# Memory attention and long convolution in one kernel: two stages in series against one program ordered by a build-time list scheduler

## The chip, the cores and the metric

One core of a Trainium2 chip runs the whole kernel. The metric is device time in microseconds (us) for one execution, smaller being better. TensorE is the matmul engine; VectorE and ScalarE do elementwise work; GpSimd does a few fills; SyncE (SP) issues every DMA transfer. In the profile these are PE (PEld for weight loads), DVE, ACT, POOL and SP.

## The reference, cut to what matters

`x` has 2048 tokens of 512 features. One branch is attention with 32 heads of 16 features in 4 segments of 512 tokens: causal softmax inside a segment, plus a linear-attention memory of the earlier segments. The other is a convolution of every feature with its own 2048-tap kernel, the sum of 128 complex exponentials. A sigmoid gate per token mixes the two.

```python
for s in range(4):
    logits = einsum('bhqd,bhkd->bhqk', qs, ks) * scale + mask      # causal
    a_dot = einsum('bhqk,bhkd->bhqd', softmax(logits), vs)
    a_mem = einsum('bhld,bhde->bhle', phi(qs), M) / (einsum('bhld,bhd->bhl', phi(qs), z)[..., None] + 1e-06)
    outs.append(g * a_mem + (1.0 - g) * a_dot)
    M, z = M + einsum('bhld,bhle->bhde', phi(ks), vs), z + phi(ks).sum(l)
a = concat(outs) @ wo
l = arange(2048).astype(bfloat16)          # lags above 256 are rounded
K = einsum('dn,dnl,dn->dl', C, exp(dt * A * l), dt * B).real
b = irfft(rfft(pad(u, 4096)) * rfft(pad(K, 4096)))[:2048] + u * Dskip
return gate * a + (1 - gate) * b           # u = x; gate = sigmoid(x . gate_w)
```

The lags `l` are rounded to bfloat16, so many of the 2048 taps of a feature's kernel are equal.

## The kernel before, in words

Each engine has a list of instructions, filled by Python code in the order in which they are to run. `EngQ.add` appends an instruction with the semaphore counts that it waits for, and `KB.dma` (L107) appends a transfer to SP's list. An engine runs its list in order. The attention is written out first, wholly, then `ssm_pipeline`.

**Loads and projections.** The constants come first in SP's list, with 32 small transfers of the output weights, and then the four transfers of `x`. L295 transposes `x`, 64 blocks of 128x128. `proj_qk` (L332, L348) and `proj_v` (L363, L374) make q, k, v and the feature-mapped k, 240 matmuls of 512 columns. L434 sums the memory of the segments.

**Attention.** 64 pairs of heads (4 segments, 4 head groups, 4 pairs) run one after the other. For a pair, `emit_qk` makes the lower triangle of the scores by 128-row blocks, 8 matmuls (L544, L559) that use 32 rows of the array each, the two heads in different row strips. `emit_exp` takes the exponential with three ACT instructions (L572 and L574 of 1024 columns, L576 of 512) and multiplies the four diagonal blocks of each head by a 0/1 mask on DVE (L582, L585). `emit_pv` makes the weighted sums, 8 matmuls with 17 columns of weights (L608), two heads in different column strips. L618 takes the result of four heads out of PSUM. The normalisation (L632 to L663) and the output projection (L674, 128 matmuls of 512 columns over a zero-padded weight) are held in a list of steps, `deferred`, and one or two of them follow each pair.

**Convolution.** `ssm_pipeline` starts its loads when the attention is done (`attn_done`). It makes the per-step factors from the parameters (L843 to L868) and the powers that squaring gives (`powers`, L908 to L922, DVE). Then it runs over 4 chunks of 128 features:

- `tables_gen`: in 4 quarters of 32 features, a table F of 65 powers and a table G of 32 powers, doubled level by level with 6 DVE instructions (L880 to L885), and a pair of matmuls per feature (L992, L996) that contracts the 128 states and gives the kernel at 65 x 32 lags. L1252 takes it out of PSUM, and L1006 and L1027 copy it to rounded lags on DVE.
- `fft_front`: 128 matmuls of 64 columns (L1068) for kernel and for `x`, the second transform level (L1099, 64 columns a matmul), the product of the two spectra (L1120 to L1124 on DVE), the first inverse level (L1137).
- `bounce_read`: the result goes to DRAM and back with another layout, six transfers a chunk. Two have 32 rows outermost, two have 31, two fill one partition each.
- `fft_back`: the last inverse level (L1190), then on DVE the skip term (L1206, L1207) and the gate (L1210, L1212, 128 columns an instruction).

```python
a1 = DV.add(lambda e: e.tensor_tensor(dst_r, src_r, mrb, ALU.mult), deps=deps)                     # L880, one of six
for c in range(4):
    ...
    gen = tables_gen(c + 1) if c + 1 < 4 else None
    ...
    fft_front(c, gen, ...)
    ...
    bounce_read(c)
fft_back(3)
```

So the tables of the next chunk run beside the transform of this one, and nothing of the convolution runs beside the attention.

Of the kernel before, what the change touches and what calls it, by code (L numbers as in the profile page):

```python
# [8 lines left out]
BF16 = mybir.dt.bfloat16  # L9
F32 = mybir.dt.float32  # L10
U16 = mybir.dt.uint16

DEBUG = {}

S = 2048; D = 512; H = 32; DH = 16; NSEG = 4; LSEG = 512; NST = 128
NEG = -30000.0
NDMA_SEMS = 48
NDUMMY = 0
HOOK = False
# [9 lines left out]
class Tok:  # L29
    __slots__ = ("sem", "val")  # L30

    def __init__(self, sem, val):
        self.sem = sem
        self.val = val


class EngQ:
    def __init__(self, name, sem):
        self.name = name
        self.sem = sem  # L40
        self.count = 0
        self.items = []

    def add(self, fn, deps=(), inc=True):
        deps = [d for d in deps if d is not None]
        tok = None
        if inc:
            self.count += 1
            tok = Tok(self.sem, self.count)
        self.items.append((deps, fn, inc))  # L50
        return tok

    def emit(self, eng):
        waited = {}
        for deps, fn, inc in self.items:
            need = {}
            for d in deps:
                if waited.get(id(d.sem), -1) >= d.val:
                    continue
                if id(d.sem) not in need or need[id(d.sem)].val < d.val:  # L60
                    need[id(d.sem)] = d
            for d in need.values():
                eng.wait_ge(d.sem, d.val)
                waited[id(d.sem)] = d.val
            if fn is None:
                continue
            ins = fn(eng)
            if inc:
                ins.then_inc(self.sem, 1)


class KB:
    def __init__(self, nc, es):
        self.nc = nc
        self.es = es
        self.block = es.enter_context(nc.Block())
        self.nsem = 0
        self.PE = EngQ("pe", self.sem("q_pe"))
        self.AC = EngQ("act", self.sem("q_act"))
        self.DV = EngQ("dve", self.sem("q_dve"))  # L80
        self.PO = EngQ("pool", self.sem("q_pool"))
        self.SP = EngQ("sp", self.sem("q_sp"))
        self.dma_toks = []
        self.dma_rr = 0

    def sem(self, name):
        self.nsem += 1
        return self.es.enter_context(self.nc.semaphore(name))

    def sb(self, name, shape, dt):  # L90
        return self.es.enter_context(self.nc.sbuf_tensor(name, shape, dt))

    def dma(self, out, in_, deps=(), q=None, slow=False):
        q = q or self.SP
        if not hasattr(self, "dpool"):
            self.dpool = [[self.sem("dp%d" % i), 0] for i in range(NDMA_SEMS)]
            self.dnext = 0
        ent = self.dpool[self.dnext % NDMA_SEMS]
        self.dnext += 1
        sem, prev_total = ent  # L100
        deps = [d for d in deps if d is not None]
        if prev_total > 0:
            deps.append(Tok(sem, prev_total))
        ent[1] = prev_total + 16
        t = Tok(sem, ent[1])
        kw = {"allow_slow_non_contiguous": True} if slow else {}
        q.items.append((deps, lambda e, o=out, i=in_, s=sem, kw=kw: e.dma_start(o, i, **kw).then_inc(s, 16), False))  # L107
        self.dma_toks.append(t)
        return t
# [7 lines left out]
    def finish(self):  # L117
        self.SP.items.append(([Tok(sm, tot) for sm, tot in self.dpool if tot > 0], None, False))
        b = self.block
        with self.nc.allow_low_precision("bf16 kernel by design"):  # L120
            self._emit_all(b)
# [1219 lines left out]
```

## Time and profile before

| | us |
|---|---|
| median of 3 runs | 1047.57 (1046.41 to 1048.4) |
| the profiled execution, first to last instruction | 1045.3 |
| PE busy | 550.2 |
| DVE busy | 683.1 |
| ACT busy | 346.7 |

The profiled span is the time from the first to the last instruction of one execution. The device time of a run holds a little more, what lies around that span; the median is 2.3 us above it. Busy is the time in which an engine has at least one instruction under way, so three engines can each be busy at the same time. [...] A row of "x512" stands for 512 instructions.

### The profile page before, as it was taken

The numbers are of one execution on the slowest core, as the hardware profiler recorded it, in microseconds if no ns is written. First come the engines' busy times: TensorE is split into PE (matmuls) and PEld (weight loads), VectorE is DVE, ScalarE is ACT, GpSimd is POOL, SyncE is SP. The second block draws the span as 40 slices with busy tenths as digits, with TensorE's granted clock in tenths as the row PEclk, the third lists the DMA queues.
The fourth block names the chain that finished last, engine by engine and source line by source line (L and its number), as shares of the span: only waits on it lengthen the run. The fifth ranks groups of instructions, "written<-read, shape, count | busy, mean of one in ns | idle before, by whom it ended". The sixth has DMA issues, their size and how long they took to land.

```text
span 1045.3 us, 14554 instructions
## 1 busy us (share of the span) xinstructions
PE 550.2 (53%) x5560; PEld 348.1 (33%) x5560; DVE 683.1 (65%) x2362; ACT 346.7 (33%) x523; POOL 7.2 (1%) x7
## 2 busy tenths in 40 slices
PE   0995687977868845000118562745546651866000
PEld 0543122322222201000107562745436551865000
DVE  0896645555555451799979997999749996422404
ACT  0761377756746301100114232322323322423000
POOL 2000000000000000000000000000000000000000
PEclk9996556585585656555655555555655655555555
DMA  3300000000000003810000000130041300512413
GB/s 99 95 1 1 1 1 1 6 16 1 6 16 1 16 6 74 263 11 1 1 0 3 1 2 1 62 43 1 1 84 38 45 1 6 92 44 58 63 28 62
DMA packets 93486, 32.63 MB, mean 31 GB/s; under 512 B 85704, under 2 KB 92488, under 8 KB 92648
## 3 DMA queue, kind: packets, MB, share of 16 engines
q1 hardware_dynamic: 93416, 31.69, 13.4%
q8 instruction: 44, 0.72, 0.3%
q14 instruction: 26, 0.21, 0.1%
HBM read 23.16 MB, written 8.53 MB: 30 GB/s over the span
## 4 chain that ended last, share of the span: by engine, by line
DVE 52%; PE 24%; ACT 10%; SPq 7%; issue 3%; DMA 3%; POOL 0%; POOLq 0%; DVEq 0%
SPq L107 7%; DVE arenaB L1027 5%; DVE arenaA L885 4%; DVE arenaA L882 4%; DVE arenaA L880 4%; ACT arenaA L572 3%; DVE arenaA L884 3%; PE psum L608 3%; ACT arenaA L574 3%; PE psum L674 3%; PE psum L544 3%; PE psum L1099 3%; DVE scr L883 2%; DVE arenaA L881 2%; DVE arenaA L1120 2%
## 5 line engine op out<-in xcount | busy, mean ns | idle before, releaser
L1137 PE MATMUL psum<-arenaC,arenaB 64*128 64x64 bf16 x528 | 20.7, 237 | 164.2 <-DVE arenaC L1124 164.2
L572 ACT ACTIVATE arenaA<-psum 128x1024 bf16<-128x1024 f32 x64 | 65.5, 1024 | 110.1 <-PE psum L544 110.1
L992 PE MATMUL psum<-arenaA 128*32 128x65 bf16 x512 | 36.3, 325 | 104.5 <-DVE arenaA L943 92.1
L608 PE MATMUL psum<-arenaA,arenaB 128*17 128x512 bf16 (+3 forms) x512 | 74.4, 435 | 16.5 <-DVE arenaA L618 16.5
L896 ACT ACTIVATE arenaC<-psum 128x512 bf16<-128x512 f32 (+1 forms) x72 | 37.9, 555 | 134.8 <-PE psum L1137 117.5
L585 DVE TENSOR_TENSOR arenaA<-arenaA,mask 128x256 bf16<-128x256 bf16 x128 | 36.9, 288 | 66.8 <-ACT arenaA L576 66.8
L1252 ACT ACTIVATE arenaA<-psum 128x455 bf16<-128x455 f32 (+1 forms) x20 | 39.3, 2062 | 106.0 <-PE psum L996 106.0
L1137 PEld LDWEIGHTS psum<-arenaC,arenaB 64*128 64x128 bf16 x528 | 15.0, 122 | 173.9 <-DVE arenaC L1124 173.9
L544 PE MATMUL psum<-arenaB 32*128 32x512 bf16 (+2 forms) x384 | 62.0, 443 | 13.4 <-ACT arenaA L574 10.2
L574 ACT ACTIVATE arenaA<-psum 128x1024 bf16<-128x1024 f32 x64 | 65.1, 1017 | 0.0
L1099 PE MATMUL psum<-arenaC,arenaB 128*128 128x64 bf16 x512 | 63.0, 288 | 0.0
L1099 PE MATMUL psum<-arenaA,arenaB 128*128 128x64 bf16 x512 | 62.5, 287 | 0.0
L1109 ACT ACTIVATE arenaC<-psum 128x512 bf16<-128x512 f32 (+1 forms) x36 | 21.4, 594 | 116.7 <-PE psum L1099 115.4
L1206 DVE TENSOR_TENSOR x4c<-x4c,dskb 128x2048 bf16<-128x2048 bf16 x4 | 4.9, 1225 | 81.7 <-DMA dskb<-in_B_Dskip_dram 81.7
L992 PEld LDWEIGHTS psum<-arenaA 128*32 128x32 bf16 x512 | 22.7, 150 | 106.7 <-DVE arenaA L943 93.0
L1099 PEld LDWEIGHTS psum<-arenaC,arenaB 128*128 128x128 bf16 x512 | 57.1, 122 | 0.0
L582 DVE TENSOR_TENSOR arenaA<-arenaA,mask 128x256 bf16<-128x256 bf16 x128 | 36.6, 286 | 30.9 <-ACT arenaA L572 30.9
L1099 PEld LDWEIGHTS psum<-arenaA,arenaB 128*128 128x128 bf16 x512 | 52.8, 121 | 4.6 <-issue 2.5
L1027 DVE SCALAR_TENSOR_TENSOR arenaB<-arenaA,qmask,arenaB 128x128 bf16<-128x128 bf16 (+2 forms) x112 | 50.1, 447 | 4.0
L880 DVE TENSOR_TENSOR arenaA<-arenaA,arenaB 128x64 bf16<-128x64 bf16 (+5 forms) x176 | 52.1, 296 | 0.0
L882 DVE TENSOR_TENSOR arenaA<-arenaA,arenaB 128x64 bf16<-128x64 bf16 (+5 forms) x176 | 52.1, 296 | 0.0
L1120 DVE TENSOR_TENSOR arenaA<-psum,arenaC 128x512 bf16<-128x512 f32 (+1 forms) x36 | 23.1, 643 | 35.0 <-PE psum L1099 32.8
(145 smaller groups left out, 1248.6 us busy)
## 6 DMA issues: line engine op xcount, KB each, us to landing
arenaB<-c_M2bd SPq DMA_DIRECT2D x1, 4224.0 KB, 16.1
scr_Vd<-arenaC SPq DMA_DIRECT2D x4, 1056.0 KB, 5.0
arenaB<-c_N SPq DMA_DIRECT2D x1, 2112.0 KB, 21.2
arenaA<-in_A_x_dram SPq DMA_DIRECT2D x4, 512.0 KB, 5.1
scr_abuf<-a_sb SPq DMA_DIRECT2D x16, 128.0 KB, 1.7
arenaA<-in_A_x_dram SPq DMA_DIRECT2D x16, 128.0 KB, 4.4
arenaB<-scr_Vd SPq DMA_DIRECT2D x8, 256.0 KB, 3.6
a4c<-scr_abuf SPq DMA_DIRECT2D x16, 128.0 KB, 4.9
```

Source lines behind the costliest of these rows:

```text
L107: q.items.append((deps, lambda e, o=out, i=in_, s=sem, kw=kw: e.dma_start(o, i, **kw).then_inc(s, 16), False))
L544: toks[which] = PE.add(lambda e, r=r, J=J, n=n, off=off, kT_src=kT_src: e.matmul(psum[:, off:off + n], lhsT=kT_src[32 * r:32 * r + 32, hg, ...
L572: tA = AC.add(lambda e, sl=sl: e.activation(pT[:, sl, 0:1024], psum[:, 0:1024], ACT.Exp, scale=0.25), deps=[qt[0]] + pt_readers[sl] + extra)
L574: tB = AC.add(lambda e, sl=sl: e.activation(pT[:, sl + 1, 0:1024], psum[:, 1024:2048], ACT.Exp, scale=0.25), deps=[qt[1]] + pt_readers[sl ...
L608: ms[which].append(PE.add(lambda e, c=c, J=J, n=n, off=off, slot=slot, h=h: e.matmul(bankf(B_ND)[32 * c:32 * c + 17, 128 * J:512], lhsT=vp ...
L880: a1 = DV.add(lambda e: e.tensor_tensor(dst_r, src_r, mrb, ALU.mult), deps=deps)
L882: a4 = DV.add(lambda e: e.tensor_tensor(dst_i, src_r, mib, ALU.mult), deps=deps)
L885: a6 = DV.add(lambda e: e.tensor_tensor(dst_i, dst_i, s2, ALU.add), deps=[a4, a5])
L992: m1 = PE.add(lambda e, o=o, dq=dq, dloc=dloc, Gr=Gr, Fr=Fr, bkm=bkm: e.matmul(bankf(bkm)[32 * dq:32 * dq + 32, o:o + 65], lhsT=Gr[:, :, d ...
L1027: tq_dv.append(DV.add(lambda e, dst=dst, src=src, gi=gi: e.scalar_tensor_tensor(dst, src, qm[:, gi:gi + 1], dst, ALU.mult, ALU.add), deps= ...
L1099: mm = PE.add(lambda e, b=b, p=p, p4=p4, c_in=c_in, c_out=c_out, rho=rho, ci=ci, ncin=len(cins): e.matmul(bankf(b)[:, 256 * c_out + 64 * p ...
L1120: d1 = DV.add(lambda e, KA=KA, n_=n_, xv=xv: e.tensor_tensor(sub_ap(T1, 0, [[256, 2], [1, n_]]), xv, sub_ap(KA, 0, [[256, 2], [1, n_]]), A ...
```

## The change

The whole kernel is written anew. Every instruction, or a closure of several matmuls, is an `Op` with an engine, a modelled cost, the tiles that it reads and writes, and a key. `Sched.schedule` runs over all of them when the kernel is built. On each engine it takes, of the ops whose inputs are there within 0.12 us, the one with the lowest key, and it so fixes one order per engine for attention and convolution together. SBUF tiles come from pools with a fixed number of buffers; a pool that lies over another's memory opens when that one has been given back. In the model a transfer costs SP 0.06 us. Keys: attention group i (of 32) has 6 + 12 i, the tables of chunk c have 50 + 70 c, the last stage starts at 335.

- **Loads**: one small constant, parameters and the first part of `x` stand first in SP's order.
- **Attention**: 32 groups of four heads. A group has five PSUM tiles of 1024 columns, each with one exponential. The diagonal is masked by a further matmul that adds -30000 to the scores; the DVE masks are gone. The memory state uses k's two feature parts as separate matmuls; normalisation works with tokens on partitions, with transposes on PE; the output projection has no padding (64 matmuls instead of 128).
- **Tables**: whole chunks of 128 features, 32 x 49 products that hold each rounded lag once, three DVE instructions a level on real and imaginary part together (15 levels, 78 steps of 256 elements a chunk), powers mostly on ACT. The kernel stays at its distinct lags: it is transposed to 5 x 128 rows, and no copy to 2048 lags is made.
- **Transform**: at odd frequencies. `x`'s first level is made early, with 32 matmuls of 512 columns, and kept in DRAM. In the last stage, 16 steps of 128 frequencies: the kernel's spectrum is a product of a constant matrix (transferred per step) with the distinct lags, 10 matmuls of 512 columns; 16 small matmuls (64x64, 256 columns, four at a time) for `x`; three products on DVE; 4 matmuls of 512 columns back; result to DRAM, and read back 4 steps at a time with 8 partitions a transfer.
- **End**: per block of 128 tokens one matmul for the skip term, two half-height ones for the last level, and one DVE instruction for the gate, 16 times.

```diff
-class EngQ:
-    def add(self, fn, deps=(), inc=True):
...
+    def schedule(self):
...
+                for key, seq, o in lst:
+                    est = te
+                    for d in o.deps:
+                        a = arrive(d, e)
+                        if a > est:
+                            est = a
...
+                    if best is None or est < best[0] - 1e-9:
+                        best = (est, key, seq, o)
+                    if est <= te + SL:
+                        best = (est, key, seq, o)
+                        break
...
+            slots = [[(Ah, 0, 0, 0), (Bh, 0, 1, 0)],
+                     [(Ah, 1, 0, 0), (Bh, 1, 1, 0), (Ah, 3, 0, 384), (Bh, 3, 1, 384)],
+                     [(Ch, 0, 0, 0), (Dh, 0, 1, 0)],
+                     [(Ch, 1, 0, 0), (Dh, 1, 1, 0), (Ch, 3, 0, 384), (Dh, 3, 1, 384)],
+                     [(Ah, 2, 0, 0), (Bh, 2, 1, 0), (Ch, 2, 0, 256), (Dh, 2, 1, 256)]]
...
+                        mm(e, ap(P, bk * 512 + off, n=n), ap(kT, 128 * J, n=128, p0=32 * r, np_=32),
+                           ap(qT, 128 * J, n=n, p0=32 * r, np_=32), len(dg[bk]) == 0, False, tile_position=(32 * r, 0))
...
+                        i = mm(e, ap(P, bk * 512 + d[0], [[st, len(d)], [1, 128]]), ap(ident, n=128),
+                               ap(negm, dims=[[0, len(d)], [1, 128]]), False, True)
...
+                op("ACT", c_act(1024), lambda e, P=P, pT=pT: e.activation(ap(pT, n=1024), ap(P, n=1024), ACT.Exp, scale=0.25), r=[P], w=[pT])
...
+                op("DVE", c_tt(256 * n), lambda e: e.tensor_tensor(
+                    D_(), ap(tile, src * 128, [[pl, 2], [128 * sstep, n], [1, 128]]),
+                    ap(pw, d0, [[0, 2], [0, n], [1, 128]]), ALU.mult), r=rd + [pw], w=wr + [tile])
...
+            for t in range(16):
+                S.key = k0 + 4 + 3.8 * t
...
+                S.dma(lambda Dt=Dt: ap(Dt, n=1280), lambda t=t: hD[t], 327680, w=[Dt], key=S.key - 8)
...
+                        for kt in range(5):
+                            i = mm(e, ap(PK, c * 512, n=512), ap(Dt, kt * 256 + c * 128, n=128), ap(KTT, kt * 512, n=512), kt == 0, kt == 4)
...
+                S.dma(lambda t=t: bass.AP(Vd, t * 131072, [[1024, 128], [1, 1024]]), lambda V=V: ap(V, n=1024), 262144, r=[V], pw=[dV[t // 4]])
+                if t % 4 == 3:
...
+                            S.dma(lambda bl=bl, c=c, k=k: sbp(V2, 64 * bl + 32 * c + k, 4, 8, [[512, 32], [1, 512]]),
...
+                op("DVE", c_dps(512), lambda e, P=P, ou=ou, aj=aj, bl=bl, b4=b4: e.scalar_tensor_tensor(
+                        ap(ou, bl * 512, n=512), ap(P, n=512), ap(omg4T, b4, n=1), ap(aj, bl * 512, n=512), ALU.mult, ALU.add),
...
+        for s in range(4):
+            for hg in range(4):
+                i0 = 8 * s + 2 * hg
...
+                for gi in range(2):
+                    S.key = TA0 + GA * (i0 + gi)
+                    group(s, hg, gi)
...
+        for c in range(4):
+            S.key = TT0 + TT * c
+            tables(c)
...
+        tail(TT0 + 4 * TT + 5)
+        S.schedule()
...
```

## Rows read from the trace of the kernel before

**Rows 1.** The page: busy time of the three engines, share of the span, instructions.

```profile
PE 550.2 (53%) x5560; PEld 348.1 (33%) x5560; DVE 683.1 (65%) x2362; ACT 346.7 (33%) x523; POOL 7.2 (1%) x7
```

**Rows 2.** The page: the chain that ended last, share of the span by engine.

```profile
DVE 52%; PE 24%; ACT 10%; SPq 7%; issue 3%; DMA 3%; POOL 0%; POOLq 0%; DVEq 0%
```

**Rows 3.** Busy time by stage: start:end, length, engines (instructions), PEclk, DMA share, GB/s.

```profile
25.50:84.00 58.50, 57.68 (x324) 28.79 (x323) 52.21 (x96) 38.45 (x68) 0.00 (x0) 1.00 0.15 47
...
112.00:405.50 293.50, 220.57 (x1252) 73.73 (x1250) 147.87 (x377) 155.39 (x192) 0.00 (x0) 0.62 0.02 7
405.50:470.00 64.50, 3.54 (x24) 2.06 (x24) 43.83 (x166) 7.84 (x12) 0.00 (x0) 0.52 0.51 135
470.00:961.70 491.70, 253.25 (x3744) 234.31 (x3744) 400.43 (x1610) 138.62 (x240) 0.00 (x0) 0.54 0.12 23
961.70:1045.30 83.60, 4.61 (x124) 2.50 (x114) 21.62 (x68) 4.78 (x8) 0.00 (x0) 0.50 0.34 64
```

**Rows 4.** Timeline of PE and SP at the start: start, length, what, idle before.

```profile
20.83 2.07 SPq L107 DMA_DIRECT2D arenaA<-in_A_x_dram  x4
...
24.95 5.79 PE L295 MATMUL psum<-ident,arenaA 128*128 128x128 bf16 x64 [24.95 <-DMA arenaA<-in_A_x_dram]
```

**Rows 5.** Groups by line and shape: exponentials and DVE instructions; busy, mean ns.

```profile
L574 ACT ACTIVATE arenaA<-psum 128x1024 bf16<-128x1024 f32 x64 | 65.1, 1017 | 0.0
L576 ACT ACTIVATE arenaA<-psum 128x512 bf16<-128x512 f32 x64 | 38.6, 603 | 0.0
L618 DVE CAST arenaA<-psum 128x512 bf16<-128x512 f32 x32 | 21.9, 684 | 0.5 <-PE psum L608 0.5
L880 DVE TENSOR_TENSOR arenaA<-arenaA,arenaB 128x1024 bf16<-128x1024 bf16 x16 | 11.0, 686 | 0.0
L1206 DVE TENSOR_TENSOR x4c<-x4c,dskb 128x2048 bf16<-128x2048 bf16 x4 | 4.9, 1225 | 81.7 <-DMA dskb<-in_B_Dskip_dram 81.7
L880 DVE TENSOR_TENSOR arenaA<-arenaA,arenaB 128x256 bf16<-128x256 bf16 x32 | 9.2, 287 | 0.0
```

**Rows 6.** Timeline of PE in the attention, first at high clock, then at low.

```profile
206.83 0.61 PE L544 MATMUL psum<-arenaB 32*128 32x512 bf16 x6
...
208.12 1.90 PE L674 MATMUL psum<-arenaC,arenaA 128*128 128x512 bf16 x8
...
258.78 1.24 PE L608 MATMUL psum<-arenaA,arenaB 128*17 128x512 bf16 x8
259.95 0.61 PE L659 MATMUL psum<-arenaB,arenaC 64*128 64x512 bf16 x1
260.67 1.03 PE L544 MATMUL psum<-arenaB 32*128 32x512 bf16 x6
261.50 0.42 PE L559 MATMUL psum<-arenaB 32*128 32x256 bf16 x2
...
393.13 3.60 PE L674 MATMUL psum<-arenaC,arenaA 128*128 128x512 bf16 x8 [0.78 <-DVE arenaA L663]
```

**Rows 7.** PE in one early stretch of the tables (L992, L996): columns as rows 3.

```profile
470.30:496.50 26.20, 2.36 (x64) 2.10 (x64) 26.20 (x130) 2.16 (x1) 0.00 (x0) 0.50 0.00 1
```

**Rows 8.** PE alone in three stretches of the attention: busy, PEclk, DMA share, GB/s.

```profile
183.40:205.50 22.10, 19.53 (x116) 0.50 0.00 1
205.50:222.50 17.00, 13.97 (x113) 0.98 0.10 32
222.50:229.30 6.80, 5.81 (x36) 0.56 0.00 0
```

**Rows 9.** DMA in two dense stretches: columns as rows 3.

```profile
20.80:34.50 13.70, 8.72 (x78) 6.62 (x79) 4.62 (x11) 6.40 (x12) 0.00 (x0) 1.00 0.86 272
416.00:436.00 20.00, 1.29 (x9) 0.69 (x8) 12.23 (x29) 6.25 (x10) 0.00 (x0) 0.50 0.85 330
```

**Rows 10.** SP's queue near the end: one chunk's six reads of the bounce.

```profile
987.47 30.53 SPq L107 DMA_DIRECT2D arenaB<-scr_Vd  x6
```

More of the change, by code (lines that the diff above doesn't have):

```diff
@@ new lines, with __init__, try_alloc, take @@
+class Pool:
+    def __init__(self, name, addr, size, n=1, phase=1):
+        self.name, self.addr, self.size, self.n, self.phase = name, addr, size, n, phase
+        self.free = [(i, ()) for i in range(n)]
+        self.left = 0
+        self.queue = []
+        self.qpos = 0
+        self.last = {}
+        self.blockers = ()
+    def try_alloc(self, tile):
+        if self.queue[self.qpos] is not tile or not self.free:
+            return None
+        prev = []
+        for b in self.blockers:
+            if b.left:
+                return None
+            for v in b.last.values():
+                prev += v
+        best = min(self.free, key=lambda f: max([o.fin for o in f[1]], default=0.0))
+        return best, prev
+    def take(self, tile, got):
+        best, prev = got
+        self.free.remove(best)
+        self.qpos += 1
+        tile.slot = best[0]
+        tile.prev = list(best[1]) + prev
+    def give(self, tile):
+        self.free.append((tile.slot, tuple(tile.users)))
+        self.last[tile.slot] = tile.users
+        self.left -= 1
@@ new lines, with __init__, register, try_alloc @@
+class Psum:
+    def __init__(self):
+        self.free = {b: () for b in range(8)}
+        self.left = 0
+    def register(self, tile):
+        pass
+    def try_alloc(self, tile):
+        w = tile.width
+        best = None
+        for i, cand in enumerate(tile.banks):
+            if all(b in self.free for b in cand):
+                t = max([o.fin for b in cand for o in self.free[b]], default=0.0)
+                if best is None or t < best[0] - 1e-9:
+                    best = (t, cand)
+        if best is None:
+            return None
+        prev = [o for b in best[1] for o in self.free[b]]
+        return (best[1], prev), []
+    def take(self, tile, got):
+        (cand, prev), _ = got
+        for b in cand:
+            del self.free[b]
+        tile.slot = cand[0]
+        tile.cand = cand
+        tile.prev = prev
+    def give(self, tile):
+        for b in tile.cand:
+            self.free[b] = tuple(tile.users)
@@ new lines, in build_kernel @@
+        mm = lambda e, o_, l, r_, st, sp, **kw: e.matmul(o_, lhsT=l, rhs=r_, start=st, stop=sp, skip_group_check=True, **kw)
+        S.tag = "load"
+        praw = []
+        prm = (B_A_re, B_A_im, B_B_re, B_B_im, B_C_re, B_C_im)
+        for wi in range(6):
+            T = Tile(prP, BF16)
+            S.dma(lambda T=T: ap(T, dims=[[128, 4], [1, 128]]), lambda wi=wi: prm[wi].rearrange("(k p) n -> p k n", p=128),
+                  131072, w=[T], key=0.1 * wi - 1)
+            praw.append(T)
@@ new lines, in sbp @@
+        def sbp(T, p0, pstep, np_, dims):
+            v = S.sb16[:]
+            st = v.ap[0][0]
+            base = (T.pool.addr + T.slot * T.pool.size) // 2
+            return bass.AP(v.tensor, v.offset + p0 * st + base, [[pstep * st, np_]] + [list(d) for d in dims])
+        S.key = 0.0
+        pb, dt, zr, zi = ssm_prep()
+        do_xT(0)
+        S.key = 6.0
+        ssm_powers(pb, dt, zr, zi)
+        S.key = 3.0
+        gates()
+        for s in range(1, 4):
+            S.key = 8.0 + s
+            do_xT(s)
```

2276 lines of the change are left out of this document (1086 added, 1190 removed).

## The prediction

> **What bounds the kernel now.** Read the busy times first: DVE is busy for 683.1 us, PE for 550.2 and ACT for 346.7, together 1580 us in a span of 1045.3 [rows 1]. No engine is full, and on average one and a half work at a time. The chain that ended last is on DVE for 52%, on PE for 24% and on ACT for 10% [rows 2], so the bound moves from engine to engine. The stages say where. In the projection PE is busy for 57.68 of 58.50 us at full clock. In the attention (293.5 us) PE has 220.6, ACT 155.4 and DVE 147.9, at a mean clock of 0.62. Then come 64.5 us in which the convolution's loads and factors are made while PE has 3.5. In the convolution (491.7 us) DVE is busy for 400.4. The last 83.6 us hold 4.6 us of PE and 21.6 of DVE, the rest being transfers [rows 3]. A stage that leans on ACT and PE is followed by one that leans on DVE; that is what running them beside each other can use.
>
> **Start.** The transposes begin at 24.95 us, 4.1 us after `x`'s first transfer was issued at 20.83 [rows 4], as 43 transfers stand ahead of it. Now two do, so PE begins at about 8 us. From there on I cost the work of each engine, at the durations of this profile.
>
> **ACT.** 160 exponentials of 1024 columns at 1.02 us are 163 us; 104 copies and feature maps of 512 at 0.60 are 62; 52 copies of 1024 at 1.02 are 53 [rows 5]; powers and factors, 64 of 512 at 0.60, 38; the tables' copies about 11. Sum 327, of which 41 in the last stage and 286 before it. The exponentials cost what they did (2.6 us for two heads); the copies taken over from DVE are hidden by PE and DVE, which have as much to do.
>
> **DVE.** A chunk's tables are 45 instructions: 21 of 2048 elements at 1.225, 12 of 1024 at 0.686, 6 of 256 at 0.287 [rows 5], and 6 of 512 for which 0.42 lies between; 38.2 us, or 153 for four. Then 126 of 512 columns at 0.684 (86 us), 20 PSUM copies of 1024, twice that row less its fixed part, 1.2 (24), 48 spectrum products at 0.686 (33), four 2048-column skip products at 2.3 (9), and about 180 short ones at some 0.3 (54). Sum 359, of which 68 in the last stage and 291 before it. The masks, the copies to rounded lags and half of the table work are gone.
>
> **PE** depends on its clock. Two heads' scores and sums take 1.29 us at the high level (206.83 to 208.12). At the low one the sums take 1.17 (258.78 to 259.95) and the scores 1.25 (260.67 to 261.92) [rows 6]. The new masks add 10 full-array matmuls of 2048 columns together a group; eight matmuls of 512 took 1.90 us high and 3.60 low [rows 6], so 0.95 or 1.80. A group of four heads is 3.53 or 6.64 us; 32 are 113 or 212. Matmuls of 512 columns: 337 before the last stage (80 or 152 us), 256 in it (61 or 115). Some 540 of 128 or 136 columns at 0.09 (64 took 5.79 [rows 4]) are 49 us high; low they are between 49 and twice that, I take 70. The tables' 1024 at 0.037 (64 in 2.36 us [rows 7]) are 38. The 256 small ones of the transform, four at a time, are 8 or 14. So PE has 280 us (high) or 472 (low) before the last stage, and 69 or 129 in it. The 1024 matmuls of the first transform level for kernel and `x` and the 1024 of the second, each of 64 columns behind its own weight load, are gone with their stage.
>
> **Which clock?** For 22.1 us of attention PE was busy for 19.53 and was granted 0.50. When the output projection came between the pairs, 17.0 us went by at 0.98, and when it stopped, 0.56 [rows 8]. The new main part mixes both kinds: projections, output projection and masks come between the groups all along, but unevenly. I put three tenths of the main work at the low price: 280 + 0.3 x 192 = 338 us. It is nearer to the middle stretch than to the first; the ends, none and all, stay for the range.
>
> **The sum.** PE is then the bound of the main part (338 against 291 and 286). Its busy share was 0.99 in the projection [rows 3] and 0.88 in the dense attention [rows 8]; I take 0.93, so 363 us. By their keys the tables end (330) when 27 of 32 groups are through, 0.84 of that: 305 us. Then the last stage may load, with 58 us of main work still to run beside it. Its PE work is 58 + 69 = 127, or 137 us at 0.93. Its transfers hide under that: 9.4 MB of constants at 330 GB/s are 28 us, 18.9 MB in pieces of 512 to 1024 bytes at 272 GB/s (the rate of `x` and the weights) are 70 [rows 9], 98 in all. If PE were faster they would be next. Behind the last step stand a write and a read of DRAM, 16 gate instructions on DVE at 0.684 (11 us) and the output. The two DRAM trips and the output are bounded by 5 us (their bytes) and 30; I take 14, so 25 together. Sum: 8 + 305 + 137 + 25 = 475 us, against the span of 1045.3. The median of the runs stands 2.3 above that span, so 477.
>
> **What waits newly.** SP has some 215 transfers in one fixed order, and the model costs each 0.06 us where the four of `x` took 0.52 each [rows 4]. A spectrum step's write waits on its PSUM copy, and behind it on SP stand the constants of a later step, for which PE waits. With three buffers of constants that is hidden as long as a step (8 us in the sum above) is longer than a trip; without that cover a trip of about 5 us a step would add up to 80.
>
> **Rivals.**
>
> *High clock throughout.* DVE is the bound of the main part: 291 / 0.93 = 313, of which 0.84 are 263; last stage (45 + 69) / 0.93 = 122; 8 + 263 + 122 + 25 = 418 us. For it: 0.98 in the middle stretch. Against it: 0.50 at 88% busy [rows 8]. [...] Chance 0.20.
>
> *Low clock throughout.* (472 + 129) / 0.93 = 646, with start and end 679 us. For it: the 0.50 of pure attention [rows 8]; against it, that the new main part is never that alone. Chance 0.04.
>
> *Little overlap.* The order is fixed from modelled costs, and every engine runs in order; where real durations differ, the engines wait for each other in turn. The new busy times are 407 (PE, mixed), 359 and 327, together 1093. The sum above has 2.3 engines busy at a time. The attention before had 1.8 (523.8 in 293.5) and the convolution 1.6 (792.3 in 491.7) [rows 3]. At 1.7, 643 us. Chance 0.10.
>
> *The last stage hangs on its transfers.* Six reads of the old bounce held SP for 30.53 us, 5.1 each [rows 10]. The new last stage has 48 that write 8 or 16 partitions; at 5.1 they are 245 us in place of the 137, total 583. For it: the same kind of detour through DRAM. Against it: the reads of `x` and weights at 272 GB/s [rows 9]. [...] Chance 0.08.
>
> *Slower than before.* The engines don't overlap: each exponential waits for its scores, the sums for it, the next scores for a PSUM pair, of which there are two, and the tables on DVE stand in the list behind a wait. Then busy times add: 1093 + 33 = 1126 us. It decides once fewer than 1.08 engines are busy at a time (1093 over 1012 us). Even the stages before had 1.6 and more. Chance 0.02, and 0.01 that the two effects meet within 0.2%.
>
> **How the numbers follow.** The forecast (mixed clock, about 430 to 540) has 0.55, and its time is the number given: 477. The range takes it in with the high-clock case (418) and the case of slow transfers (583), together 0.83; with the bounds of the clock and of the end it runs from 410 to 620. Outside lie little overlap, low clock and slower. The three runs differ by 0.2%, about what can be told from no change. Faster by more than that: 0.97; within it: 0.01; slower: 0.02.
>
> **What would show it.** In the new profile: first transposes before 10 us; DVE near 360, ACT near 330 and PE between 350 and 450 us busy; instructions of both branches mixed on DVE until about 300 us; mean clock 0.7 to 0.9; a last stage of about 160 us in which PE leads and transfers move some 200 GB/s. The prediction is wrong in its main step if PE is not the engine that the chain follows in the main part, and in its last if PE stands waiting on transfers there.

## The result and the profile after

The rewritten kernel takes 589.95 us (median of 4 runs, 588.37 to 592.4) against 1047.39 us before in the same comparison: a ratio of 0.563, 95% interval [0.561, 0.565]. Where a median below and a ratio differ, the ratio leaves out disturbed executions, of which the profiled one of experiment 8 (498.37 us) is one. The sign and the range held. The time given, 477, was 113 us too low, and what follows is mostly about these 113 us.

Lines that the text names: L715 is every matmul, L758 the transposes of `x`, L1030 the exponentials, L1191 the copy of the table products out of PSUM, L1097 a copy of the attention's result, L991 and L992 parts of the feature map (DVE, SBUF only), L1145 to L1151 the three table instructions, L1199 the kernel's rows after their trip through DRAM, L1282 and L1284 the copies that are written to `scr_V`, L1320 the gate, L248 every transfer. (Kernels with added lines are off by one to four.)

The page of the kernel after, busy times and the chain by engine; they answer to [rows 1] and [rows 2].

```profile
PE 451.5 (76%) x3837; PEld 225.3 (38%) x3837; DVE 377.3 (64%) x569; ACT 371.7 (63%) x405; POOL 5.0 (1%) x17
...
PE 28%; DVE 22%; ACT 18%; DMA 18%; SPq 9%; issue 4%; DVEq 0%; ACTq 0%
```

The three engines together are busy for 1200 us in 590.6, 2.0 at a time instead of 1.5. But ACT has 371.7 where the sum had 327, and DVE 377 instead of 359: the instruction counts are as read from the diff, so single instructions must have become longer.

Busy time by stage of the kernel after, as in [rows 3]. PEclk is the clock that TensorE was granted, as a share of full speed; each of the 40 clock records in the trace of before, and of the 40 in that of after, is 0.50 or 1.00, so a value between them is a mean over the stretch. The stages are the powers, the gate's trip through DRAM, the main part up to the last table, the last stage up to its last product, the drain.

```profile
29.50:67.90 38.40, 19.85 (x196) 10.78 (x195) 25.14 (x46) 34.41 (x61) 0.49 (x2) 0.63 0.00 1
67.90:88.60 20.70, 11.38 (x74) 4.12 (x72) 9.24 (x15) 9.26 (x12) 0.00 (x0) 0.75 0.17 27
88.60:413.00 324.40, 283.68 (x2596) 151.42 (x2595) 247.37 (x343) 237.18 (x227) 2.65 (x8) 0.75 0.19 31
...
413.30:545.00 131.70, 101.60 (x801) 45.56 (x799) 63.03 (x114) 68.16 (x76) 0.00 (x0) 0.89 0.82 180
545.00:590.60 45.60, 14.31 (x48) 3.52 (x48) 15.40 (x18) 0.77 (x2) 0.00 (x0) 0.65 0.48 124
```

The tables end at 413 us; the prediction had 8 + 305 = 313. From there to the last product it takes 132 us (predicted 137), and the drain 46 (predicted 25). So 100 of the missing time lie before 413 us and 21 in the drain.

The longest groups of ACT and DVE in the kernel after, by line and shape (busy us, mean ns); the exponential and the 512-column copy have their counterparts in [rows 5].

```profile
L1030 ACT ACTIVATE sb<-psum 128x1024 bf16<-128x1024 f32 x160 | 189.3, 1236 | 42.5 <-PE psum L715 41.4
L1191 ACT ACTIVATE sb<-psum 128x392 bf16<-128x392 f32 x16 | 32.6, 2108 | 3.5 <-PE psum L715 3.5
L1097 DVE CAST sb<-psum 128x512 bf16<-128x512 f32 x16 | 28.6, 1790 | 9.6 <-PE psum L715 9.6
L991 DVE TENSOR_SCALAR sb<-sb 128x512 bf16<-128x512 bf16 x12 | 11.5, 962 | 0.0
```

The same exponential took 1017 ns before. A mean hides how that comes about; the smallest, median and largest duration of one group show it (ns).

```profile
L1030 ACT ACTIVATE sb<-psum x160: 1000/1023/9067, 25.3 to 464.3; 128x1024 bf16<-128x1024 f32 x160
```

Most are as before, and a few last up to nine times as long. The timeline says when: one burst of table matmuls.

```profile
149.58 0.75 DVE L986 TENSOR_SCALAR sb<-psum,sb 128x512 bf16<-128x512 f32 x1 [8.65 <-ACT sb L985]
149.94 9.60 ACT L1191 ACTIVATE sb<-psum 128x392 bf16<-128x392 f32 x4
150.25 8.40 DVE L991 TENSOR_SCALAR sb<-sb 128x512 bf16<-128x512 bf16 x1
150.38 8.19 PEld L715 LDWEIGHTS psum<-sb 128*32 128x32 bf16 x128 [1.82 <-DVE sb L986]
150.38 11.88 PE L715 MATMUL psum<-sb 128*32 128x49 bf16 x143 [1.54 <-DVE sb L986]
158.89 0.45 DVE L1158 COPY sb<-sb 128x256 bf16<-128x256 bf16 x1 [0.24 <-PE psum L715]
```

128 table matmuls take 8.19 us, 0.064 each where [rows 7] gave 0.037, both at the granted clock of 0.50 (here from 150.40 to 158.60 us). For almost that whole time ACT and DVE have one instruction each under way: ACT one of the four in its row (8.46 us), DVE one that does 512 elements from SBUF to SBUF (its median is 0.28 us). Both end when the burst ends. The new tables are read by PE in steps of 128 elements, 256 bytes; the old ones in steps of 64 bytes, and in the kernel before no table instruction of DVE (L880 to L885) took over 0.69 us.

### The profile page after: what moved, and what is told of

It reads as the page before. It is cut to its first block, busy times and chain, and to the rows that moved or that the text cites. A ratio compares the mean times of both kernels' runs of the same rounds, so it can differ in the third digit from the quotient of the medians.

```text
span 590.6 us, 9127 instructions
## 1 busy us (share of the span) xinstructions
PE 451.5 (76%) x3837; PEld 225.3 (38%) x3837; DVE 377.3 (64%) x569; ACT 371.7 (63%) x405; POOL 5.0 (1%) x17
## 4 chain that ended last, share of the span: by engine, by line
PE 28%; DVE 22%; ACT 18%; DMA 18%; SPq 9%; issue 4%; DVEq 0%; ACTq 0%
PE psum L715 27%; SPq L248 9%; ACT sb L1030 6%; DMA scr_V<-sb 5%; ACT sb L1191 5%; DVE sb L1151 5%; DMA scr_K<-sb 4%; DVE sb L1148 4%; DVE sb L1145 4%; DMA sb<-scr_K 2%; DMA scr_gbuf<-sb 2%; DMA sb<-scr_V 2%; DVE sb L1282 1%; DVE sb L879 1%; DMA sb<-in_A_wq_dram 1%
## 5 line engine op out<-in xcount | busy, mean ns | idle before, releaser
L715 PE MATMUL psum<-sb 128*32 128x49 bf16 (+12 forms) x3601 | 432.2, 384 | 115.7 <-ACT sb L1030 24.2
L715 PEld LDWEIGHTS psum<-sb 128*128 128x128 bf16 (+5 forms) x3601 | 207.2, 155 | 335.1 <-issue 123.7
L1030 ACT ACTIVATE sb<-psum 128x1024 bf16<-128x1024 f32 x160 | 189.3, 1236 | 42.5 <-PE psum L715 41.4
L1148 DVE TENSOR_TENSOR sb<-sb 128x2048 bf16<-128x2048 bf16 (+3 forms) x60 | 50.7, 844 | 3.1 <-PE psum L1206 3.1
L1151 DVE TENSOR_TENSOR sb<-sb 128x2048 bf16<-128x2048 bf16 (+3 forms) x60 | 51.0, 850 | 1.8
L1145 DVE TENSOR_TENSOR sb<-sb 128x2048 bf16<-128x2048 bf16 (+3 forms) x60 | 50.4, 845 | 0.1
L1191 ACT ACTIVATE sb<-psum 128x392 bf16<-128x392 f32 x16 | 32.6, 2108 | 3.5 <-PE psum L715 3.5
L1097 DVE CAST sb<-psum 128x512 bf16<-128x512 f32 x16 | 28.6, 1790 | 9.6 <-PE psum L715 9.6
L1113 ACT ACTIVATE sb<-psum,sb 128x512 bf16<-128x512 f32 x16 | 10.9, 687 | 35.6 <-DMA scr_abuf<-sb 20.8
L1246 ACT ACTIVATE sb<-psum 128x1024 bf16<-128x1024 f32 x16 | 16.4, 1023 | 22.5 <-PE psum L715 22.5
L1320 DVE SCALAR_TENSOR_TENSOR sb<-psum,sb 128x512 bf16<-128x512 f32 x16 | 10.9, 744 | 23.5 <-DMA sb<-scr_abuf 18.5
L1044 ACT ACTIVATE sb<-psum 128x512 bf16<-128x512 f32 x32 | 19.1, 596 | 5.8 <-PE psum L715 5.7
L1263 ACT ACTIVATE sb<-psum 128x1024 bf16<-128x1024 f32 x16 | 16.2, 1020 | 7.1 <-PE psum L715 3.7
L1282 DVE CAST sb<-psum 128x1024 bf16<-128x1024 f32 x8 | 9.8, 1221 | 15.8 <-DMA scr_V<-sb 12.2
L986 DVE TENSOR_SCALAR sb<-psum,sb 128x512 bf16<-128x512 f32 x16 | 11.8, 745 | 9.0 <-ACT sb L985 8.9
L982 ACT ACTIVATE sb<-psum 128x512 bf16<-128x512 f32 x16 | 9.5, 596 | 11.0 <-PE psum L715 11.0
L1284 ACT ACTIVATE sb<-psum 128x1024 bf16<-128x1024 f32 x8 | 8.2, 1024 | 11.0 <-PE psum L715 5.6
L985 ACT ACTIVATE sb<-psum,sb 128x512 bf16<-128x512 f32 x16 | 10.9, 684 | 6.5 <-PE psum L715 6.4
L877 ACT ACTIVATE sb<-psum 128x1024 bf16<-128x1024 f32 x8 | 8.2, 1025 | 10.2 <-PE psum L715 10.2
L934 DVE CAST sb<-psum 128x512 bf16<-128x512 f32 x16 | 14.0, 884 | 0.9 <-PE psum L715 0.9
```

What stands on the lines that cost most here:

```text
L715: mm = lambda e, o_, l, r_, st, sp, **kw: e.matmul(o_, lhsT=l, rhs=r_, start=st, stop=sp, skip_group_check=True, **kw)
L1030: op("ACT", c_act(1024), lambda e, P=P, pT=pT: e.activation(ap(pT, n=1024), ap(P, n=1024), ACT.Exp, scale=0.25), r=[P], w=[pT])
L1044: op("ACT", c_act(512), lambda e: e.activation(ap(raw, n=512), ap(PV, n=512), ACT.Copy), r=[PV], w=[raw])
L1097: op("DVE", c_dps(512), lambda e: e.tensor_copy(ap(oT, n=512), ap(P3, n=512)), r=[P3], w=[oT])
L1145: op("DVE", c_tt(256 * n), lambda e: e.tensor_tensor(D_(), ap(tile, src * 128, [[pl, 2], [128 * sstep, n], [1, 128]]), ap(pw, d0, [[0, 2], ...
L1148: op("DVE", c_tt(256 * n), lambda e: e.tensor_tensor(T_(), ap(tile, pl + src * 128, [[-pl, 2], [128 * sstep, n], [1, 128]]), ap(pw, sg[0] ...
```

## Experiments

Twelve kernels. The comparisons are made by the ratio to the kernel before, which ran beside each.

**1. The tables' row pitch.** Rows of 132 elements instead of 128, so that PE steps by 264 bytes. The order on every engine stays.

```diff
-            FPL, GPL = 32 * 128, 49 * 128
+            TP = 132; FPL, GPL = 32 * TP, 49 * TP
...
-  ... ap(F, cc * FPL + dl, [[128, 32]]), ap(G, cc * GPL + dl, [[128, 49]]), ...
+  ... ap(F, cc * FPL + dl, [[TP, 32]]), ap(G, cc * GPL + dl, [[TP, 49]]), ...
...
-        dskbT = S.keep(2048, F32)
+        dskbT = S.keep(1024, BF16)
```

> The tables of powers are stored with rows of 132 instead of 128 features, so that the matmuls that contract them step through memory by 264 bytes instead of 256; the order on every engine is the same (to make room the skip factors are kept in bfloat16 and a pool of small tiles has 6 buffers instead of 8). Theory A, the step of 256 bytes hits the same part of SBUF each time and shuts the other engines out: the 8 to 10 us instructions on ACT and DVE beside the table matmuls vanish, 128 table matmuls take about 5 us instead of 9, and the time falls from 590 to 500 to 540 us. Rival B, any step over a few elements does it: time and the long instructions stay, 585 to 595 us. Rival C, it is not the reads (small matmuls in column strips, or PSUM): the same as B here.

528.34 us, ratio 0.504 [0.501, 0.506]: 62 us less. The exponentials of this kernel, and its copies of the products:

```profile
L1030 ACT ACTIVATE sb<-psum x160: 1000/1024/1084, 24.9 to 406.9; 128x1024 bf16<-128x1024 f32 x160
...
L1191 ACT ACTIVATE sb<-psum x16: 497/498/503, 142.0 to 356.7; 128x392 bf16<-128x392 f32 x16
```

None of these is long any more (1.08 and 0.50 us at most), and the last table product is copied at 357 us instead of 413. ACT is busy for 312.7 us and DVE for 332.4, near the 327 and 359 of the sum. PE falls from 451.5 to 385.2.

**2. Consecutive elements instead of a step.**

```diff
-  ... ap(F, cc * FPL + dl, [[128, 32]]), ap(G, cc * GPL + dl, [[128, 49]]), ...
+  ... ap(F, cc * FPL + 32 * dl % 4064, [[1, 32]]), ap(G, cc * GPL + 48 * dl, [[1, 49]]), ...
```

> The 1024 table matmuls read consecutive elements of the tables instead of one in 128 (the kernel of the convolution is then wrong; as many matmuls of the same shape, order and place). A and B both say: no long instructions on ACT or DVE beside them, a burst of 128 in about 5 us, 500 to 540 us in all. C says: 585 to 595 us, the long instructions stay. Together with the run at 264 bytes this parts A from B.

This kernel contracts other elements of the tables, so its convolution is not the reference's. 525.43 us, ratio 0.501 [0.499, 0.503], level with the first; and as it has none of the first's other edits, those made nothing of the gain. So it is the 256-byte step that costs the kernel time; the step of 264 bytes costs it next to nothing (528.34 against 525.43 us). For PE itself that step does not look free. Here are the 1024 table matmuls of the kernel after and of the first experiment's:

```profile
L715 PE MATMUL psum<-sb 128*32 128x49 bf16 x1024 | 67.9, 499 | 2.8 <-DVE sb L986 1.5 <-ACT sb L982 1.2
...
L715 PE MATMUL psum<-sb 128*32 128x49 bf16 x1024 | 27.0, 280 | 0.0
```

That is 0.066 us each against 0.026. With consecutive elements a stretch of 69 matmuls that begins with them takes 0.72 us, 0.010 each (timeline of PE at 139.17 us); no row has all 1024 of that kernel. The clocks differ too: stretches with table matmuls were granted 0.50 in the kernel after (229.00 to 240.50 and 398.00 to 413.00 us) and 1.00 in the first experiment (345.00 to 357.00), so a part of the 67.9 against 27.0 can be the clock's (as in [rows 6]). What holds the other engines in this case is the 256-byte step: the longest exponential takes 9.07 us with it, and 1.08 us with 264 bytes as with consecutive elements.

**3. Which of the two operands?** G, the moving one, gets rows of 132; F, the weights, keeps 128.

```diff
-            FPL, GPL = 32 * 128, 49 * 128
+            TPF, TPG = 128, 132; FPL, GPL = 32 * TPF, 49 * TPG
```

> Only the table G (the moving operand of the table matmuls, 49 columns) has rows of 132 elements; F (the weights, 32 columns) keeps 128, so that the weights are still read in steps of 256 bytes. Theory J (the moving operand's step holds the other engines): as with both changed, 523 to 535 us, and no exponential over 1.2 us. Theory K (the weights' step does): 575 to 595, with single instructions of 8 to 10 us. If both add to it: 550 to 575.

543.25 us, ratio 0.518 [0.515, 0.521]: between theory J and the case that both add to it. The exponentials of this kernel:

```profile
L1030 ACT ACTIVATE sb<-psum x160: 999/1024/4082, 26.5 to 418.6; 128x1024 bf16<-128x1024 f32 x160
```

Some are still held, for 4.08 us instead of 9.07 at the longest. The moving operand's step makes 47 of the 62 us and the weights' step, mended after it, the other 15 (0.518 against 0.504). Rows of 132 for F alone were not tried.

**4. Is PE the bound of the main part?** The 320 mask matmuls are left out, first in the kernel as it is, then with rows of 132.

```diff
-                        i = mm(e, ap(P, bk * 512 + d[0], [[st, len(d)], [1, 128]]), ap(ident, n=128), ap(negm, ...), False, True)
```

> The 320 matmuls that add the causal mask are left out (so the attention isn't causal); the order of everything else is the same. If PE is the bound of the main part, as the prediction's sum has it, 30 us (high clock) to 58 us (low clock) of PE work go, and the time falls by at least 25 us. If other engines and waits set the pace, it falls by less than 12 us. A lower clock for want of full-array matmuls could even add up to 10 us.

> The kernel with rows of 132 elements without its 320 mask matmuls; it leaves out the causal mask of the attention. The order on all engines is the same otherwise. The masks are 30 us of PE work at the high clock and 58 at the low. Theory H (with the long instructions gone, PE is the bound of the main part, as the prediction had it): at least 20 us less than 528, so 508 or below. Rival I (the main part goes at the pace of scores, exponential and sums waiting for one another, no engine being full): 516 to 530.

578.56 us, 0.552 [0.551, 0.554], 11 us less than the rewrite; and with rows of 132, 527.7 us, 0.504 [0.502, 0.505], no less at all. Here is the same stretch with the masks (first kernel, rows of 132) and without:

```profile
88.00:357.00 269.00, 224.85 (x2564) 106.08 (x2582) 205.50 (x342) 176.30 (x224) 2.65 (x8) 0.87 0.21 36
```

```profile
88.00:357.00 269.00, 212.12 (x2407) 97.33 (x2406) 208.71 (x352) 178.77 (x232) 2.78 (x8) 0.81 0.24 40
```

PE, the busiest engine, has 12.7 us less to do, at a mean granted clock of 0.81 where it was 0.87; that the lower clock took back part of what was removed is not shown. The two others do hardly more in the time (3.2 us on DVE, 2.5 on ACT). So PE was not the bound of this kernel's main part, and with no engine full the next thing to look for is something serial.

**5. The trip of a chunk's kernel through DRAM.** In the kernel with rows of 132 the chain has pieces such as these (start, us):

```profile
138.49 8.11 PE psum L715 x246
147.14 11.81 DMA scr_K<-sb
158.97 2.89 DMA sb<-scr_K
```

The table products leave PE, go to DRAM and come back in another layout, 14.7 us, and the next chunk's tables begin behind that. The diff shows why: the small tile that takes them (`kl`, L1199) comes from the pool of three buffers that the table products use (`t2P`), and buffers are given out in the order of the program. In the kernel of this experiment `kl` has memory of its own. The edit also doubles what the scheduler's model charges per packet, so that it puts such a trip at 12.3 us (4096 packets) instead of 6.1. The two were not tried apart.

```diff
-        pTP = mkpool("pT", 2048, 8)
+        pTP = mkpool("pT", 2048, 7)
...
+        klP = mkpool("kl", 1280, 1)
-            kl = Tile(t2P, BF16)
+            kl = Tile(klP, BF16)
-        lat = max(nbytes / 290e3, packets * 0.0015)
+        lat = max(nbytes / 290e3, packets * 0.003)
```

> The kernel with rows of 132 elements, in which the small tile that takes the kernel's rows after their trip through DRAM (L1199) has memory of its own (one of the eight tiles of exponentials makes room) instead of one of the three buffers of the table products; so the next chunk's tables no longer queue behind it. The scheduler's price of a packet is 0.003 instead of 0.0015 us. With rows of 132 the chain has, between 88 and 357 us, three such trips: 14.7, 14.5 and 14.5 us from the write's issue to the read's landing, in which DVE does some 3 us of work each. Theory P (the main part follows the chain tables, table matmuls, trip, next tables): about 3 x 11 us less than 528, 490 to 508. Rival Q (the trips are hidden by the attention, or PE, busy for 225 of these 269 us, takes over at once): 518 to 532.

504.77 us, ratio 0.481 [0.479, 0.482]: 24 us less than with the pitch alone, as theory P had it. The three trips with the shared buffers (length, then PE, PEld, DVE, ACT busy):

```profile
147.50:161.90 14.40, 12.42 (x122) 6.19 (x118) 2.42 (x7) 10.02 (x13) 0.00 (x0) 1.00 0.96 86
215.70:229.90 14.20, 13.95 (x131) 6.55 (x131) 7.19 (x17) 9.82 (x13) 0.65 (x1) 1.00 0.71 58
287.20:301.30 14.10, 12.67 (x125) 5.66 (x122) 5.60 (x16) 11.63 (x14) 0.00 (x0) 1.00 0.72 60
```

and with `kl` by itself:

```profile
147.00:161.40 14.40, 14.40 (x140) 6.53 (x135) 13.73 (x25) 12.16 (x15) 0.00 (x0) 1.00 0.95 76
203.70:217.50 13.80, 13.80 (x108) 5.92 (x108) 13.08 (x27) 9.60 (x12) 0.66 (x1) 1.00 0.74 59
268.30:282.50 14.20, 13.81 (x144) 5.98 (x136) 13.77 (x27) 11.76 (x15) 0.00 (x0) 1.00 0.92 77
```

The trips are as long as before. DVE now works 40.6 us in them instead of 15.2: 25 more, about as much as the time has fallen. PE is busy for 42.0 of their 42.4 us. The main part of this kernel, to be held against the 224.85 of 269.00 us in experiment 4:

```profile
88.00:332.00 244.00, 222.77 (x2597) 103.28 (x2594) 204.24 (x342) 178.19 (x226) 2.79 (x8) 0.90 0.27 50
```

With the pitch and the trips mended, PE is busy for 0.91 of the main part, and the chain of the whole span is on PE for 40%, against 28% in the kernel after.

**6. The gate's trip.** From 67.9 to 88.6 us the rewrite is half idle (stage rows above): the gate goes to DRAM and back, and DVE waits in its list for it, with tables queued behind.

```profile
73.15 1.22 DVE L1145 TENSOR_TENSOR sb<-sb 128x2048 bf16<-128x2048 bf16 x1
84.23 0.17 DVE L914 TENSOR_SCALAR sb<-sb 128x16 f32<-128x16 f32 x1 [9.87 <-DMA sb<-scr_gbuf]
```

```diff
-  ... bass.AP(gbuf, i, [[64, 32], [4, 16]]), 2048, r=[dG], pw=[g4T], slow=True)
+  ... bass.AP(gbuf, i, [[64, 32], [4, 16]]), 2048, r=[dG], pw=[g4T], slow=True, key=150)
-  op("DVE", 0.2, lambda e: e.tensor_scalar(ap(omg4T, n=16), ...), r=[g4T], w=[omg4T])
+  op("DVE", 0.2, lambda e: e.tensor_scalar(ap(omg4T, n=16), ...), r=[g4T], w=[omg4T], key=320)
```

> The reading back of the token gates and the DVE instruction on them get later keys (150 and 320 instead of 20), so that neither SP nor DVE stands behind the 12 us write of the gates at 68 to 89 us; the scheduler moves some neighbours too. If that stall is on the path: 10 to 20 us less. If the engines catch up later, or the write is waited for by something else (the output projection's first copies need nothing of it): within 5 us.

581.19 us, ratio 0.555 [0.553, 0.556], 8.7 us less: nearly the whole 9.87 us of that wait, though less than the 10 to 20 us that were expected.

**7. The last stage: SP's price, and more buffers for `scr_V`.** Both on the kernel with rows of 132.

```diff
-        return self.op("SP", 0.06, lambda e: e.dma_start(out(), in_(), **kw), ...)
+        return self.op("SP", 0.55, lambda e: e.dma_start(out(), in_(), **kw), ...)
```

> The kernel with rows of 132 elements, and the scheduler's price of a transfer on SP raised from 0.06 to 0.55 us. All orders are made anew; in SP's list the last chunk's read of scr_K then stands behind 13 of the 32 reads of scr_Z instead of all of them, and most loads of x and of the attention's result behind the writes of scr_V. Theory D (the last stage starts late and halts because SP's order was made with a price of 0.06 us): scr_K's read is issued about 12 us earlier and the writes of scr_V land sooner; 508 to 520 us against 528. Rival E (the data have to come through the same queues anyway, so their order changes nothing): 524 to 533.

```diff
-        VP = mkpool("V", 2048, 2, 2)
+        VP = mkpool("V", 2048, 4, 2)
```

> The kernel with rows of 132 elements, and four buffers instead of two for the tile that a spectrum step writes to DRAM (scr_V). In the profile with two, DVE stands 11.1 us and ACT 5.1 us at the copies into that tile until an earlier write has landed, and the chain has 17.7% of its last 172 us on these writes, 30 us. Theory F (two buffers are too few for writes that take 8 to 10 us to land): 512 to 521 us against 528. Rival G (what counts is when the last write has landed and is read back; the waits move there): 524 to 533.

The first gave 530.39 us, with executions from 524.0 to 537.7, in which no difference can be told; its scr_K read was issued at 370.33 instead of 390.23 us, and the end did not move. The second gave 526.57, ratio 0.503 [0.502, 0.503], about 1.4 us less, with intervals that overlap: theory G. With four buffers the waits for `scr_V` are gone, and the chain of its last 170 us has 12% on the constants `c_D` instead. Each wait there had another right behind it.

**8. The edits together.** The kernel of experiment 5 with the gate's keys, SP's price, four buffers for `scr_V` and six for the constants.

```diff
-        DP = mkpool("Dst", 2560, 3, 2)
+        DP = mkpool("Dst", 2560, 6, 2)
```

> The same as e9_kl, and with it: SP's price 0.55 us, four buffers for the tiles written to scr_V, six instead of three for the constants c_D, and the gate's read-back at a later key (150, its use 320 instead of 20). Theory P2 (each of these only pays once the trips of the main part are gone, and the last stage is a chain of transfers that deeper buffers cover): 15 to 30 us less than e9_kl. Rival R (the last stage is held by what its transfers move, 28 MB at some 180 GB/s being 155 us, whatever the buffers): within 10 us of e9_kl, most of that the gate's.

Ratio 0.468 [0.466, 0.471] (median 495.86 us), against 0.481 for experiment 5: 13 us less. That lies between the two theories. 8.7 us of it would be the gate's, if that is worth here what it was in experiment 6; the rest of the set would be 4 us, and which of it was not tried. This is the fastest version, with the last one below.

**9. The reads of `scr_Z` ahead of the last trip.** SP's queue in the kernel of experiment 8:

```profile
328.89 0.37 SPq L248 DMA_DIRECT2D scr_K<-sb  x1
329.30 35.66 SPq L248 DMA_DIRECT2D sb<-scr_Z  x32
365.00 1.31 SPq L248 DMA_DIRECT2D sb<-in_A_x_dram  x2
366.36 0.43 SPq L248 DMA_DIRECT2D sb<-scr_K  x1
```

The last chunk's trip takes 37 us, for 32 reads stand in it; the three before it have 11.1 to 11.7 us between write and read. Now 24 of the 32 wait behind it.

```diff
-                              131072, r=[dZ], pw=[zparts[zq]], key=k0 + zq)
+                              131072, r=[dZ] + ([kds[3]] if zq else []), pw=[zparts[zq]], key=k0 + zq)
```

> The same as e10_all, with 24 of the 32 reads of scr_Z made to wait in SP's list until the last chunk's kernel rows have been read back. In e10_all SP takes 35.66 us for the 32 reads between the write of scr_K (328.89) and its read (366.36), where the three trips of the main part have 11.1 to 11.7 us there. Theory S (the last stage's first products wait for this trip, and behind them all 16 steps): the read is issued some 20 us earlier, and since the attention's end still takes part of the engines until 385 us, 8 to 20 us less than e10_all (495.9), 476 to 488. Rival T (the steps then wait for scr_Z or for the engines instead, and the end does not move): 491 to 499.

500.02 us, ratio 0.477 [0.476, 0.479]: 9.5 us more, which neither theory had. SP and DVE in this kernel:

```profile
354.14 0.43 SPq L248 DMA_DIRECT2D sb<-scr_K  x1
...
358.71 20.77 SPq L248 DMA_DIRECT2D sb<-scr_Z  x24
```

```profile
387.83 0.69 DVE L1271 TENSOR_TENSOR sb<-sb 128x1024 bf16<-128x1024 bf16 x1 [19.77 <-DMA sb<-scr_Z]
```

The kernel's rows are there 12 us earlier, two steps run, and then DVE waits 19.77 us for `scr_Z`. The steps hang on the reads, wherever these stand. In the kernel of experiment 8 the stretch from 332 to 366 us reads

```profile
332.00:366.00 34.00, 27.00 (x302) 12.60 (x294) 11.82 (x31) 25.57 (x30) 0.00 (x0) 1.00 1.27 154
```

with the DMA engines taken up throughout (their packets' time adds up to 1.27 of the stretch) at 154 GB/s. The prediction had used 272 for these pieces [rows 9]. What keeps the rate at 154 was not tried.

**10. The drain.** Experiment 9 with four buffers instead of two for the tiles that bring the attention's result back.

```diff
-        ajP = mkpool("aj", 4096, 2, 2)
+        ajP = mkpool("aj", 4096, 4, 2)
```

> The same as e11_zx, with four buffers instead of two for the tiles that bring the attention's result back for the end (scr_abuf). In e10_all SP waits at 442.57 to 447.99 for the attention's last write before it reads those tiles, and the last write of scr_V, whose data are there at about 446.5, is issued only at 451.67; later the gate instructions wait 5.6 us for buffers of the output, whose transfers stand behind the second half of these reads. Theory U (the drain hangs on SP's list): 5 to 11 us less than e11_zx. Rival V (the drain is the trip of the last step's data through DRAM and the gate instructions, about 45 us, wherever the reads stand): within 3 us of e11_zx.

490.24 us, ratio 0.471 [0.468, 0.473]: 7 us less than experiment 9, theory U. With the ratio of experiment 8 it is level (the intervals overlap). Without the edit of experiment 9 it wasn't tried; since that edit cost 9.5 us, it may be faster still. SP's end in this kernel has no reads of the attention's result left in it:

```profile
441.26 9.88 SPq L248 DMA_DIRECT2D scr_V<-sb  x4
452.87 2.75 SPq L248 DMA_DIRECT2D sb<-scr_V  x4
473.20 10.83 SPq L248 DMA_DIRECT2D out_dram<-sb  x16
```

## Why the prediction was right in kind and 113 us too low

**Start: right.** The first transposes begin at 5.65 us, below the 10 that were named (kernel after, timeline of PE):

```profile
5.65 1.03 PE L758 MATMUL psum<-sb 128*128 128x128 bf16 x8 [1.39 <-DMA sb<-in_A_x_dram]
```

**Busy sums: right, but for what no row showed.** With the pitch mended, DVE has 332 us (359 predicted), ACT 313 (327), PE 385 (350 to 450 was named). The instruction counts and the prices of [rows 5, 6] carried over from one kernel to a wholly different one.

**"The tables' 1024 at 0.037 are 38": the step that failed most.** It took a price from [rows 7] for matmuls of the same kind and did not ask whether their operands lie in the same steps. They cost 0.064 each, and worse, while they run the other two engines stand inside an instruction. Experiments 1 to 3 show it: 62 us in the median, 56 of them in the time at which the tables end (413 against 357).

**"PE is then the bound of the main part": failed.** The prediction named this as its main step and said what would show it wrong: that the chain does not follow PE there. Experiment 4 shows it by the time: 320 matmuls taken out, which leaves PE 12.7 us less busy in that stretch, and no change. The main part was a chain of tables, products, trip and next tables. A trip of each chunk's kernel through DRAM was in the diff, but in the prediction trips stand in the last stage only. "What waits newly" looked at SP and not at who holds which buffer. Experiment 5 shows the 24 us. The bound of the projection (PE 0.99 busy, [rows 3]) was no guide to a part in which three engines wait in turn. Once these waits are gone the step comes near to true: PE is then busy for 0.91 of the main part, where 0.93 was taken, and the chain of the whole span is on PE for 40% instead of 28%. That PE bounds it there was not tried by taking work out.

**The gate's trip** was costed at nothing, and without being named: 8.7 us (experiment 6). It is the same mechanism, an engine that runs in order waiting for DRAM with other work queued behind.

**The clock: about right.** Three tenths of the main work at the low price were assumed. The mean granted clock from 88 to 357 us is 0.87 with the pitch mended, so, with records of 0.50 and 1.00 only, 0.26 of the time at the low level; with the 256-byte step it is 0.75 from 88.6 to 413, half the time. In the burst of table matmuls at 229 to 241 us PE was busy for 11.76 of 12.00 us and was granted 0.50:

```profile
229.00:241.00 12.00, 11.76 (x175) 10.85 (x176) 11.25 (x5) 8.84 (x3) 0.52 (x2) 0.50 0.01 3
```

**The last stage: the sum was right by luck.** 132 us against 137 up to the last product. But PE was busy for 101.6 of them, where the sum had 127, and idle for 30, where it had 10. Transfers do not "hide": in this stretch ACT stands 22.4 us and DVE 16.0 us until one has landed. At 154 to 180 GB/s the 28.3 MB of the sum take 157 to 184 us instead of 98, and experiments 7 and 9 gained nothing, the waits going from one transfer to the next. Two errors, too much work for PE and too little waiting for transfers, cancelled. The rival of slow transfers had the right place and a price too high (5.1 us a read; four reads of `scr_V` take SP 2.75).

**"Behind the last step: 25": mis-sized.** 45.6 us. PE waits 15.16 us for the read of `scr_V`, and SP takes 23.69 us to issue 12 reads of the attention's result: before the last four it stands 17.2 us, until the gate instructions (L1320) have given a buffer back (kernel after, SP's queue):

```profile
547.26 2.75 SPq L248 DMA_DIRECT2D sb<-scr_V  x4
550.11 23.69 SPq L248 DMA_DIRECT2D sb<-scr_abuf  x12
573.84 2.09 SPq L248 DMA_DIRECT2D out_dram<-sb  x4
```

Together: 100 late at the tables' end, 5 early in the last stage, 21 late in the drain, 116 against a span forecast of 475, which was 590.6. Of the 100 the pitch made 56, the chunks' trips 26 (357 to 330.3 us, last table copy in experiment 5), the further edits of the last kernels 6 (324.5 in experiment 10); 12 are not shown. About 10 of those may be more work done by then, an estimate: when the tables end, 139 of the 160 exponentials are through, 0.87 where the sum had 0.84 of the main work, and 0.03 of its 363 us is 10. The mended kernels, at 490 to 496 us, come within 13 to 19 us of the forecast.

**The rivals.** Little overlap (643 us, 1.7 engines at a time) was the nearest in kind, with 2.0 measured; its mechanism, engines waiting in turn, was at work, but with two places that could be named. Of the rest none happened: the clock was neither high nor low throughout, and nothing came near slower.

## What to carry to other kernels

When a price is taken over for an instruction of the same shape, compare the steps in bytes of its operands too, and look at the smallest, median and largest duration of the neighbours on the other engines, not at means. Where a chunk's data go through DRAM and come back, ask which buffer the returning data need and whose work is queued behind it in the same pool and on the same engine: that, and no engine's busy time, set the pace here until it was mended. Removing one wait in a chain of transfers was worth nothing here (experiment 7), since the transfer behind it was as late.

## What the runs showed of the hardware that was not expected

The table matmuls that read in steps of 256 bytes hold single instructions of ACT and DVE, the longest for 8 to 10.5 us (kernel after: a copy of the products 8.46, an exponential 9.07, a copy of the attention's result 10.55), also one that reads and writes SBUF alone (L991, 8.40). With 264 bytes the longest of the first three take 0.50, 1.08 and 0.69 us, and L991 takes 0.28 in the mean; with consecutive elements the three take 0.53, 1.08 and 0.69. The same 1024 matmuls keep PE busy for 67.9 us at 256 bytes and 27.0 at 264, at granted clocks that differ. The step of the moving operand weighs more (47 us, mended first) than that of the weights (15 us). That the step hits the same part of SBUF each time, as theory A has it, no run shows; whether other multiples of 256 do the same was not tried.
